# Denominators of linear attention by heads in column groups, their reciprocals spread over features by DMA through DRAM

## The chip, the cores and the metric

One core of one Trainium2 chip runs the kernel. The metric is device time in microseconds (us) of one execution, as the median over several runs; less is better. A profile taken by the hardware gives one execution in detail: its span goes from the first to the last instruction.

## What is computed

x is 2048 rows of 512 features, bfloat16. Two blocks follow each other, each with a layernorm ahead and x added behind: linear attention with 32 heads of 16 features, and a dense layer with 1792 hidden features and a relu.

```
qkv = (x @ wqkv)               # x after layernorm; 32 heads of Dh = 16
phi = lambda t: where(t > 0, t + 1, exp(t)) + 1e-6
pq, pk = phi(q), phi(k)
kv  = einsum("bhsd,bhse->bhde", pk, v)
z   = einsum("bhsd->bhd", pk)
num = einsum("bhqd,bhde->bhqe", pq, kv)
den = einsum("bhqd,bhd->bhq", pq, z)[..., None] + 1e-6
o   = num / den
h   = x + o @ wo
h2  = h + relu(layernorm(h) @ w1) @ w2
```

There is one denominator for each row and head, and it divides the 16 features of that head.

## The kernel before

The rows are cut into 16 tiles t of 128 rows, four of which make a block c of 512 rows (four blocks, c = 0 to 3; the text calls them blocks 1 to 4). All intermediates stay in SBUF. PSUM is one tensor `bk` of eight banks, and every step names its banks itself.

The kernel's body is a set of small functions `op_...`, and a text `ORDER` that lists them one after the other with their indices: `K.8.0` calls `op_K(8, 0)`, tile 8 into bank 0. The order of the words is the order in which each engine gets its instructions; there is no other scheduler. Engines run their own instructions in this order and wait for each other by semaphores. All DMAs are issued by SyncE (SP in the profile), also in this order, so a DMA whose data are late holds up the DMAs behind it.

The steps, with their lines in the kernel before:

- `lx`, `lk`, `lq`, `lv`, `lo`, `l1`, `l2` (L198, L201): loads of x and the weights. `warm` (L212): matmuls on zeros at the start. `S`, `A` (L215, L216): layernorm statistics on VectorE; `R` (L221, L222): one over the standard deviation by Ln and Exp on ScalarE; `N` (L229): the normalised tile, on VectorE.
- The normalised tile is needed transposed, in `lnT`: for tiles 0 to 5 by TensorE (`T`, L248) with a copy by ScalarE (`E`, L258) or VectorE (`V`, L261), for the others by a transposing DMA (`X`, L269).
- `K` (L277): keys of a tile; `F`, `U` (L295, L298): Exp and Relu from PSUM on ScalarE, two tiles at a time; `M`, `D` (L302, L305): minimum, add on VectorE, which give phi(k). `Q`, `qF`, `qU`, `qM`, `qD` do the same for the queries of a block, transposed (`pqT`), in four parts jb of 128 features, that is 8 heads.
- `G` (L329): x^T phi(k), summed over all tiles in banks 4 to 7; `z` (L337): the sums of phi(k); then `gD`, `gA` (L357, L354) copy G, `kv` (L362) multiplies with the value weights, `kx` (L370) masks it to heads, `m` (L374) multiplies with wo, `mD` (L380) copies it to `m_sb`. `zc` (L343) copies z; `zh` (L346) spreads it into `zhd`, 32 columns for each jb, of which 8 are the heads of that jb; `zr` (L351) spreads it into `zrep`, 128 columns, where each head's column stands 16 times.
- Denominators of block 1: `d4` (L386) makes four matmuls of 128x32 by 128x512, one for each jb, into four groups of 32 partitions of one bank: one row for each head. `dl4`, `dx4` (L392, L397) take one over it as Exp(-Ln). `rp` (L402) repeats it 16 times by four matmuls with `erep`, `rm` (L408) multiplies `pqT` with it from PSUM into `pqs`.
- Denominators of blocks 2 to 4: `d` (L415) makes one matmul of 128x128 by 128x512 for each jb with `zrep`, whose result stands repeated already; `dl`, `dx` (L418, L423) take one over it, one pass each for each jb, and `dm` (L426) multiplies `pqT` with it into `pqs`.
- `h` (L435): pqs times m_sb; `hD` (L441) adds x. `s`, `a`, `r`, `n` (L217, L218, L221, L236): statistics of the second layernorm; `t`, `x`: transposes by TensorE or by DMA (L270).
- `p` (L450): the hidden features f of a block; `pA`, `pD` (L456, L461): relu from two banks, on ScalarE or VectorE. `f` (L470): the second dense product of a tile; `fo` (L478): scaling and adding h; `fd` (L485): the store.

Around the change the order runs, on TensorE: the last Q and G, z, kv, m and the block 1 denominators, then h of block 1 mixed with Q of blocks 3 and 4, then p of block 1, and in it d of block 2. The d of blocks 3 and 4 come later, ahead of p of blocks 2 and 3.

Of the kernel before, what the change touches and what calls it, by code (L numbers as in the profile page):

```python
# [57 lines left out]
def kernel(  # L58
# [366 lines left out]
    def op_dm(c, jb):  # L425
        nc.vector.tensor_tensor(  # L426
            out=pqs[:, (c * KD + jb) % NQ, :], in0=pqT[c][:, jb, :], in1=rd[:, jb, :], op=ALU.mult
        )
# [92 lines left out]
```

## Time and profile before

| | us |
|---|---|
| median of 3 runs | 174.51 |
| the runs | 174.51, 175.42, 174.1 |
| span of the profiled execution | 173.1 |
| TensorE, VectorE, ScalarE, GpSimd busy in it | 165.8, 99.7, 72.3, 4.7 |
| first dense row of matmuls starts (K.0) | 8.71 |
| last matmul ends, by the chain | 170.06 |

The profile names no device time of its own for the profiled execution; what there is of it is the span, which lies 1.4 us under the median and 1.0 to 2.3 under the three runs. The granted TensorE clock was 1.000 over the span. PE is TensorE's matmuls, PEld its weight loads, DVE VectorE, ACT ScalarE, POOL GpSimd, SPq the issuing of DMAs by SyncE. A group's line has the source line, engine, operation, tiles and shapes, then total and mean time, then the idle time of its engine ahead of it and what ended that. Matmul durations (379 ns for 512 columns) overlap; their spacing in a dense row is read from the chain. The chain goes back from the last instruction to what released each step.

### The profile page before, as it was taken

Reading aid. Unit: us, or ns where it says so; the run is one execution under the profiler, and the core shown is the slowest. Engines: PE = TensorE matmul, PEld = TensorE weight load, DVE = VectorE, ACT = ScalarE, POOL = GpSimd, SP = SyncE. Lnnn points to the kernel's source line nnn. Section 1 sums busy time; section 2 is a strip of 40 time slices with the busy share of each in tenths; the row PEclk is TensorE's granted clock in tenths of the full one; section 3 lists DMA queues with packets and bytes.
Section 4 is the critical chain, followed back from the end, with each engine's and each line's share of the span. In section 5 each row is a group of like instructions: output and inputs, shape, how many; then the busy total and the mean of one; then the engine's idle time right before and its main releaser. Section 6 shows DMA issues by size and latency. Waiting matters only on the chain.

```text
span 173.1 us, 2263 instructions
## 1 busy us (share of the span) xinstructions
PE 165.8 (96%) x856; PEld 77.7 (45%) x872; DVE 99.7 (58%) x208; ACT 72.3 (42%) x112; POOL 4.7 (3%) x21
## 2 busy tenths in 40 slices
PE   7699989999999999999999999999999999999992
PEld 2244434446444544444444444444444444444551
DVE  3899965154799949796338089455769402500032
ACT  2499755666586794213057210006623000363100
POOL 7300000000000000000000000000000000000000
PEclk9999999999999999999999999999999999999999
DMA  5883456899000000002220000462001320010021
GB/s 139 280 307 61 77 132 152 255 364 360 4 0 0 4 0 0 0 0 61 61 64 30 0 2 0 108 78 91 0 0 30 65 60 0 30 62 0 0 80 45
DMA packets 19979, 13.00 MB, mean 75 GB/s; under 512 B 12544, under 2 KB 18816, under 8 KB 19968
## 3 DMA queue, kind: packets, MB, share of 16 engines
q1 hardware_dynamic: 19968, 12.85, 26.5%
q8 instruction: 7, 0.11, 0.3%
q14 instruction: 4, 0.03, 0.1%
HBM read 7.86 MB, written 2.10 MB: 58 GB/s over the span
## 4 chain that ended last, share of the span: by engine, by line
PE 85%; DVE 7%; DMA 5%; issue 1%; SPq 1%
PE bk L470 28%; PE bk L450 28%; PE bk L435 8%; PE bk L285 8%; PE bk L329 5%; PE bk L277 4%; DVE st L215 4%; DMA lnT<-h_nat 2%; DMA x_nat<-in_A_x_dram 2%; DVE h_nat L229 2%; PE bk L415 2%; PE bk L337 1%; DVE eb L302 1%; PE bk L374 1%; PE bk L248 1%
## 5 line engine op out<-in xcount | busy, mean ns | idle before, releaser
L450 PE MATMUL bk<-lnT,w_sb 128*128 128x512 bf16 x220 | 50.9, 379 | 0.2
L470 PE MATMUL bk<-w_sb,at 128*128 128x512 bf16 (+1 forms) x233 | 49.8, 366 | 0.3
L470 PEld LDWEIGHTS <-at 128*128 128x128 bf16 x238 | 23.3, 98 | 25.3
L450 PEld LDWEIGHTS <-w_sb 128*128 128x128 bf16 x224 | 21.9, 98 | 26.5
L456 ACT ACTIVATE at<-bk 128x1024 bf16<-128x1024 f32 x14 | 14.2, 1022 | 41.0 <-PE bk L450 22.3
L478 DVE SCALAR_TENSOR_TENSOR gT<-bk,rstd,h_nat 128x512 bf16<-128x512 f32 (+1 forms) x17 | 11.8, 716 | 30.4 <-PE bk L470 17.0
L461 DVE TENSOR_SCALAR at<-bk 128x1024 bf16<-128x1024 f32 x14 | 17.1, 1221 | 14.4 <-PE bk L450 14.4
L295 ACT ACTIVATE eb<-bk 128x1024 bf16<-128x1024 f32 (+1 forms) x18 | 16.6, 930 | 10.4 <-PE bk L277 6.1
L418 ACT ACTIVATE ld<-bk,eps 128x512 f32<-128x512 f32 x12 | 7.7, 693 | 27.7 <-PE bk L415 27.7
L298 ACT ACTIVATE rb<-bk 128x1024 bf16<-128x1024 f32 (+1 forms) x18 | 16.6, 927 | 1.3 <-DVE pqs L408 0.7
L277 PE MATMUL bk<-wk_sb,lnT 128*128 128x512 bf16 x64 | 15.3, 379 | 0.6 <-DMA lnT<-h_nat 0.6
L441 DVE TENSOR_TENSOR h_nat<-bk,x_nat 128x512 bf16<-128x512 f32 x16 | 10.7, 682 | 8.6 <-PE bk L435 8.6
L435 PE MATMUL bk<-m_sb,pqs 128*128 128x512 bf16 x62 | 15.2, 379 | 0.1
L285 PE MATMUL bk<-lnT,wq_sb 128*128 128x512 bf16 x61 | 14.7, 379 | 0.1
L329 PE MATMUL bk<-at,h_nat 128*128 128x512 bf16 x55 | 13.2, 379 | 0.1
L215 DVE BATCH_NORM_STATS2 st<-x_nat 128x6 f32<-128x512 bf16 x16 | 10.5, 680 | 2.7 <-DMA x_nat<-in_A_x_dram 2.7
L302 DVE TENSOR_SCALAR eb<-eb 128x1024 bf16<-128x1024 bf16 (+1 forms) x18 | 6.9, 389 | 7.0 <-ACT eb L295 7.0
L217 DVE BATCH_NORM_STATS2 st<-h_nat 128x6 f32<-128x512 bf16 x16 | 10.7, 683 | 0.2
L435 PEld LDWEIGHTS <-pqs 128*128 128x128 bf16 x64 | 6.3, 98 | 7.5
L277 PEld LDWEIGHTS <-lnT 128*128 128x128 bf16 x64 | 6.1, 98 | 7.9 <-DMA lnT<-h_nat 1.0
L329 PEld LDWEIGHTS <-h_nat 128*128 128x128 bf16 x64 | 6.2, 98 | 7.3
L285 PEld LDWEIGHTS <-wq_sb 128*128 128x128 bf16 x64 | 6.0, 98 | 6.9 <-issue 0.2
(63 smaller groups left out, 95.2 us busy)
## 6 DMA issues: line engine op xcount, KB each, us to landing
w_sb<-in_B_w_dram SPq DMA_DIRECT2D x4, 896.0 KB, 8.1
out_dram<-gT SPq DMA_DIRECT2D x15, 128.0 KB, 1.8
x_nat<-in_A_x_dram SPq DMA_DIRECT2D x2, 512.0 KB, 7.0
x_nat<-in_A_x_dram SPq DMA_DIRECT2D x3, 256.0 KB, 4.0
wk_sb<-in_A_wqkv_dram SPq DMA_DIRECT2D x2, 256.0 KB, 4.8
wq_sb<-in_A_wqkv_dram SPq DMA_DIRECT2D x2, 256.0 KB, 6.8
wv_sb<-in_A_wqkv_dram SPq DMA_DIRECT2D x2, 256.0 KB, 3.3
wo_sb<-in_A_wo_dram SPq DMA_DIRECT2D x2, 256.0 KB, 8.9
```

The source lines that it names most:

```text
L215: op_S = lambda t: nc.vector.bn_stats(out=st[:, t, :], in_=x_nat[:, t, :])
L277: nc.tensor.matmul(bk[:, b, :], lhsT=lnT[c][:, kd, j * P : (j + 1) * P], rhs=wk_sb[:, kd, :], start=(kd == 0), stop=(kd == KD - 1),)
L285: nc.tensor.matmul(bk[:, b, :], lhsT=wq_sb[:, kd, j * P : (j + 1) * P], rhs=lnT[c][:, kd, :], start=(kd == 0), stop=(kd == KD - 1),)
L295: nc.scalar.activation(out=buf(eb, kind, i, n), in_=bank(at_bank[kind, i], n), func=ACT.Exp)
L298: nc.scalar.activation(out=buf(rb, kind, i, n), in_=bank(at_bank[kind, i], n), func=ACT.Relu)
L329: nc.tensor.matmul(bk[:, KD + kd, :], lhsT=ln_nat[:, t, kd * P : (kd + 1) * P], rhs=pk(t)[:, 0, :], start=(t == 0), stop=(t == NT - 1),)
L435: nc.tensor.matmul(bk[:, b, :], lhsT=pqs[:, (c * KD + jb) % NQ, j * P : (j + 1) * P], rhs=m_sb[:, jb, :], start=(jb == 0), stop=(jb == KD ...
L450: nc.tensor.matmul(bk[:, b, :], lhsT=w1_sb[:, kd, f * P : (f + 1) * P], rhs=lnT[c][:, kd, :], start=(kd == 0), stop=(kd == KD - 1),)
L456: nc.scalar.activation(out=acts[c % 2][:, f : f + n, :], in_=bank(at_bank["p", c, f], n), func=ACT.Relu)
L461: nc.vector.tensor_scalar(out=acts[c % 2][:, f : f + n, :], in0=bank(at_bank["p", c, f], n), scalar1=0.0, scalar2=None, op0=ALU.max,)
L470: nc.tensor.matmul(bk[:, b, 0 : w * P], lhsT=acts[c % 2][:, f, j * P : (j + 1) * P], rhs=w2_sb[:, f, k * P : (k + w) * P], start=(f == 0), ...
L478: nc.vector.scalar_tensor_tensor(out=o_t[:, t % NO, cols], in0=bk[:, at_bank["f", t, k], 0 : w * P], scalar=rstd2[:, t : t + 1], in1=h_nat ...
```

## The change

For blocks 2 to 4 the four `d`, `dl`, `dx` of a block are replaced by one `d4`, one `dl4` and one `dx4`, as block 1 has them. The reciprocals go to `r4`, which is the memory of `wk_sb` (the key weights, no longer needed by then). Four DMAs `rw` write each head's row 16 times into a DRAM tensor `scr`, 128 KB each; two DMAs `rr` read two jb each, 256 KB, back into `rd`, now one row for each feature; and `dm` multiplies two jb at once. An `rr` waits on SP for the two `rw` that it reads. `zr` goes. Block 1 keeps `rp` and `rm`, with its four `rp` in two pairs. The order of all engines is written anew: tile 0 is normalised ahead of the statistics of tiles 2 and 3, X goes out in the order 6, 7, 9, 8, 13, 12, 10, 11, 15, 14, `lo` is loaded in part earlier and `lq` in part later, `lv` after all X, three of four z stand directly ahead of kv, d4.0 directly behind kv, some evictions change between ScalarE and VectorE (17 `pA` and 11 `pD` where there were 14 of each), and h of blocks 3 and 4 comes ahead of p of block 2. The loads of the first 4 us keep their order. The other functions that the diff adds are called nowhere in the order.

The diff, cut to what is spoken of (of the order, the first part and the end; line numbers of the later file are those of after):

```diff
-table const masks warm.9.7 lx.0.1 S.0 lx.1.1 S.1 A.0 A.1 lx.2.2 S.3 S.2 R.1.1 R.0.1 lx.4.2 lk.0.2 lk.2.2
-lx.6.2 A.3 A.2 N.0.2.2 N.0.0.2 N.1 R.2.2 N.2 N.3 warm.1.7 T.0.3.2.2 T.0.0.0.2 T.1.1 T.2.2 E.0.2.2 E.1 V.0.0.2
-T.3.3 E.2 E.3 K.0.0 S.4 S.5 A.4 A.5 K.1.1 K.3.3 K.2.2 F.0.1 R.4.2 U.0.1 F.1.1 S.6 S.7 M.0.1 A.7 A.6 N.4 R.6.2
-U.1.1 lx.8.4 T.4.0 D.0.1 G.0 M.1.1 N.5 N.7 T.5.1 E.4 U.2.1 F.2.1 E.5 F.3.1 U.3.1 K.4.0 D.1.1 S.9 N.6 S.8 G.1
-M.2.1 A.9 A.8 D.2.1 R.8.2 K.5.1 F.4.2 U.4.2 M.3.1 S.10 N.8 D.3.1 N.9 M.4.2 S.11 D.4.2 lq.2.2 lq.0.2 lx.12.4
-A.11 A.10 X.7 X.6 X.9 X.8 lv.0.2 G.2 K.7.3 K.6.2 G.3 F.6.2 R.10.2 U.6.2 S.12 S.13 M.6.2 N.11 N.10 A.13 A.12
-D.6.2 R.12.2 G.4 G.5 K.9.1 K.8.0 F.8.2 U.8.2 S.14 N.13 A.14 N.12 S.15 M.8.2 A.15 D.8.2 X.11 X.10 R.14.2 N.14
-N.15 lv.2.2 X.12 X.13 X.14 X.15 l1.0.2 l2.0.7 l2.7.7 lo.2.2 lo.0.2 l1.2.2 G.6 G.7 K.11.3 K.10.2 F.10.2 U.10.2
-G.8 G.9 K.12.0 K.13.1 F.12.2 U.12.2 M.10.2 D.10.2 G.10 K.14.2 K.15.3 F.14.2 M.12.2 M.14.2 D.12.2 Q.0.1.1
-Q.0.0.0 G.11 G.12 qF.0.0.2 qU.0.0.2 U.14.2 G.13 Q.0.3.1 Q.0.2.0 qM.0.0.2 D.14.2 qD.0.0.2 G.14 G.15 z.1.2
-qF.0.2.2 qU.0.2.2 gD.0.2 z.0.2 z.2.2 z.3.2 zc qM.0.2.2 gA.2.2 zr zh qD.0.2.2 Q.1.1.3 Q.1.0.2 qF.1.0.2 qU.1.0.2
-kv.1.4 kv.0.4 kv.2.4 kv.3.4 kx qM.1.0.2 Q.1.3.1 m.1.5 m.0.4 d4.0.3 m.3.7 m.2.6 Q.1.2.0 Q.2.0.2 dl4.0 mD.0.2
...
-d.1.1.5 qU.3.0.2 qF.3.0.2 e.0 d.1.0.4 d.1.3.7 qF.3.2.2 qU.3.2.2 dl.1.0 v.2 p.0.0.2 d.1.2.6 p.0.1.3 p.0.2.0
-p.0.3.1 dl.1.1 dx.1.0 dx.1.1 pD.0.0.2 p.0.4.2 p.0.5.3 qM.2.2.2 pD.0.2.2 p.0.6.0 p.0.7.1 dl.1.2 pD.0.4.2 dl.1.3
-dx.1.2 dx.1.3 r.0.4 p.0.8.2 p.0.9.3 pA.0.8.2 dm.1.2 dm.1.0 dm.1.3 dm.1.1 h.6.6 h.4.4 h.5.5 qM.3.2.2 qM.3.0.2
-pD.0.6.2 p.0.13.3 p.0.10.0 h.7.7 hD.6 f.2.6.0.7 p.0.11.1 p.0.12.2 hD.5 s.5 qM.2.0.2 f.1.5.0.7 s.6 hD.4 s.4
-pA.0.10.2 qD.2.0.2 a.4 pA.0.12.2 hD.7 a.5 f.3.7.0.7 f.1.5.7.7 n.4 qD.2.2.2 a.6 n.5 n.6 s.7 a.7 qD.3.0.2 n.7
...
+const lx.0.1 S.0 lx.1.1 A.0 table R.0.1 S.1 lx.2.2 N.0.0.2 N.0.2.2 A.1 S.2 R.1.1 warm.9.7 T.0.3.2.2 warm.1.7
+T.0.0.0.2 S.3 E.0.0.2 E.0.2.2 N.1 A.3 A.2 lx.4.2 lk.0.2 S.5 R.2.2 N.2 lk.2.2 T.1.3 E.1 A.5 S.4 K.0.0 T.2.7
+K.1.6 N.3 A.4 F.0.1 lx.6.2 E.2 T.3.4 R.4.2 M.0.1 S.7 N.5 K.2.2 T.5.7 E.3 U.0.1 S.6 N.4 D.0.1 A.6 lx.8.4 lq.0.2
+lo.2.2 lx.12.4 F.1.1 K.3.3 T.4.0 U.1.1 M.1.1 A.7 E.5 R.6.2 G.0 D.1.1 S.9 F.2.1 E.4 N.6 S.8 N.7 A.8 M.2.1 A.9
+F.3.1 M.3.1 U.2.1 R.8.2 X.6 K.5.1 G.1 U.3.1 K.4.0 D.2.1 N.9 F.4.2 U.4.2 G.2 K.6.2 D.3.1 S.12 S.13 N.8 M.4.2
+A.13 A.12 S.10 D.4.2 X.7 G.3 R.12.2 K.7.3 N.13 S.11 F.6.2 U.6.2 masks X.9 M.6.2 A.10 N.12 A.11 K.9.1 G.4 X.8
+X.13 lq.2.2 X.12 K.8.0 G.5 D.6.2 G.6 R.10.2 S.15 U.8.2 F.8.2 S.14 N.10 M.8.2 N.11 A.14 D.8.2 A.15 G.7 X.10
+K.13.1 K.12.0 R.14.2 X.11 G.8 K.10.2 K.11.3 F.12.2 U.12.2 U.10.2 F.10.2 N.14 N.15 M.10.2 Q.0.1.1 D.10.2 M.12.2
+X.15 Q.0.0.0 G.9 X.14 l2.0.7 lv.2.2 lo.0.2 K.14.2 G.10 K.15.3 lv.0.2 qF.0.0.2 qU.0.0.2 l1.0.2 G.11 Q.0.2.0
+Q.0.3.1 l2.7.7 l1.2.2 F.14.2 U.14.2 M.14.2 D.12.2 D.14.2 qM.0.0.2 qU.0.2.2 qF.0.2.2 z.2.2 G.12 G.13 G.14 G.15
+z.0.2 z.1.2 z.3.2 qM.0.2.2 qD.0.0.2 gD.0.2 qD.0.2.2 zc gA.2.2 kv.0.4 kv.1.4 kv.2.4 kv.3.4 zh d4.0.6 Q.1.0.2
+dl4.0 kx m.1.5 m.0.4 dx4.0 m.3.7 m.2.6 Q.1.1.3 mA.0.2 mD.2.2 rp.0.1.5 rp.0.0.4 qU.1.0.2 qF.1.0.2 Q.1.2.0
+rp.0.2.6 rp.0.3.7 Q.1.3.1 Q.2.1.3 rm.0.0.2 qF.1.2.2 rm.0.2.2 qM.1.0.2 qD.1.0.2 qM.1.2.2 h.2.4 Q.2.0.2 h.3.5
+qU.1.2.2 qD.1.2.2 hD.2 d4.1.0 h.0.7 Q.2.3.1 h.1.4 dl4.1 s.2 hD.3 s.3 dx4.1 qF.2.0.2 qU.2.0.2 a.2 a.3 n.3 t.3.6
+e.3 hD.0 n.2 hD.1 rw.1.1 rw.1.0 Q.2.2.0 qU.2.2.2 qF.2.2.2 s.0 s.1 a.0 Q.3.1.3 Q.3.0.2 t.2.4 rw.1.3 rw.1.2 n.0
+t.0.5 qU.3.0.2 qF.3.0.2 Q.3.3.1 qM.2.0.2 a.1 n.1 v.2 t.1.6 v.0 rr.1.0.2 v.1 qM.2.2.2 Q.3.2.0 qF.3.2.2 qD.2.0.2
+dm.1.0.2 p.0.1.3 rr.1.2.2 qU.3.2.2 p.0.0.2 dm.1.2.2 qM.3.0.2 qD.2.2.2 qM.3.2.2 h.6.5 p.0.3.1 p.0.2.0 d4.2.4
+r.0.4 pD.0.0.2 dl4.2 qD.3.2.2 qD.3.0.2 h.5.6 p.0.4.2 dx4.2 pA.0.2.2 d4.3.4 dl4.3 dx4.3 p.0.5.3 p.0.6.0 p.0.7.1
+h.7.7 h.4.4 rw.2.0 rw.3.2 rw.2.1 rw.2.2 pD.0.4.2 hD.5 pD.0.6.2 hD.7 rw.2.3 rr.2.0.2 rw.3.0 rw.3.1 rr.2.2.2
+hD.4 s.7 s.4 hD.6 a.7 p.0.8.2 p.0.9.3 p.0.10.0 f.3.7.0.7 pD.0.8.2 p.0.13.3 p.0.12.2 p.0.11.1 f.1.5.0.7
+dm.2.0.2 n.7 pD.0.10.2 dm.2.2.2 rw.3.3 x.7 rr.3.0.2 rr.3.2.2 pA.0.12.2 f.3.7.7.7 h.11.3 h.10.2 hD.11 hD.10
+s.10 s.5 a.4 dm.3.2.2 dm.3.0.2 a.5 s.6 fo.3 a.6 n.4 f.2.6.0.7 f.1.5.7.7 h.9.1 n.6 hD.9 n.5 x.6 f.2.6.7.7
+h.13.2 h.15.0 h.14.1 s.11 hD.14 fo.2 hD.15 f.0.4.0.7 h.8.3 h.12.6 x.4 x.5 p.1.13.1 p.1.12.0 pA.1.12.2 s.9 s.15
...
+f.12.4.0.7 fd.11 fd.10 f.15.7.0.14.0.2 f.13.5.0.7 f.14.6.0.7 f.13.5.7.7 f.12.4.7.7 f.14.6.7.7 fd.8 fo.15.0.2
+fo.12 fo.13 f.15.4.0.14.2.2 fo.14 fd.12 fd.13 fd.15.0.2 fd.14 fo.15.2.2 fd.15.2.2
 """
...
+    dram = ctx.enter_context(tc.tile_pool(name="dram", bufs=1, space=bass.MemoryType.DRAM))
...
     o_t = gT
+    r4 = wk_sb
+    scr = dram.tile([NCH, KD, P, CW], BF16, name="scr")
...
     def op_dx4(c):
-        nc.scalar.activation(out=rd[:, c % 2, :], in_=ld[:, c % 2, :], func=ACT.Exp, scale=-1.0)
+        nc.scalar.activation(out=r4[:, c, :], in_=ld[:, c % 2, :], func=ACT.Exp, scale=-1.0)
+
+    def op_rw(c, jb):
+        src = r4[jb * Q4 : jb * Q4 + P // DH, c, :].rearrange("q (o n) -> q o n", o=1)
+        nc.sync.dma_start(
+            out=scr[c, jb].rearrange("(q r) n -> q r n", r=DH),
+            in_=src.broadcast_to([P // DH, DH, CW]),
+        )
+
+    def op_rr(c, jb, n):
+        nc.sync.dma_start(
+            out=rd[:, jb : jb + n, :], in_=scr[c, jb : jb + n].rearrange("j p n -> p j n")
+        )
 
     def op_rp(c, jb, b):
         at_bank["rp", c, jb] = b
         rows = slice(jb * Q4, (jb + 1) * Q4)
         nc.tensor.matmul(
-            bk[:, b, :], lhsT=erep[rows, :], rhs=rd[rows, c % 2, :], start=True, stop=True
+            bk[:, b, :], lhsT=erep[rows, :], rhs=r4[rows, c, :], start=True, stop=True
...
-    def op_dm(c, jb):
+    def op_dm(c, jb, n=1):
+        i = (c * KD + jb) % NQ
         nc.vector.tensor_tensor(
-            out=pqs[:, (c * KD + jb) % NQ, :], in0=pqT[c][:, jb, :], in1=rd[:, jb, :], op=ALU.mult
+            out=pqs[:, i : i + n, :], in0=pqT[c][:, jb : jb + n, :], in1=rd[:, jb : jb + n, :],
+            op=ALU.mult,
         )
 
```

More of the change, by code (lines that the diff above doesn't have):

```diff
@@ L130 @@
     rstd = big.tile([P, NT], F32, name="rstd")
+    nmean = big.tile([P, NT], F32, name="nmean")
     st2 = big.tile([P, NT, nc.vector.BN_STATS_DIM], F32, name="st2")
@@ L222, in rstd_of, with op_ng, op_Np @@
         nc.scalar.activation(out=dst, in_=dst, func=ACT.Exp, scale=-0.5)
+    def op_ng(t, n):
+        nc.gpsimd.tensor_scalar(
+            out=nmean[:, t : t + n], in0=mv[:, t : t + n, 0], scalar1=-1.0, scalar2=None, op0=ALU.mult
+        )
+    def op_Np(t):
+        nc.gpsimd.tensor_scalar(
+            out=ln_nat[:, t, :], in0=x_nat[:, t, :],
+            scalar1=nmean[:, t : t + 1], scalar2=rstd[:, t : t + 1], op0=ALU.add, op1=ALU.mult,
+        )
     op_R = lambda t, n: rstd_of(rstd[:, t : t + n], mv[:, t : t + n, 1])
@@ L332, in op_G, with op_za, op_zf, op_z @@
             )
-    def op_z(jb, b):
+    def op_za(t):
+        first = pk(0, 2) if t == 2 else z_acc
+        nc.vector.tensor_tensor(out=z_acc, in0=first, in1=pk(t, 2), op=ALU.add)
+    def op_zf(t):
+        z0, z1 = z_acc[:, 0, :], z_acc[:, 1, :]
+        nc.vector.tensor_tensor(out=z0, in0=z0, in1=z1, op=ALU.add)
+        nc.vector.tensor_copy(out=acts[1][:, 4, :], in_=z0)
+        nc.vector.tensor_tensor(out=acts[1][:, 5, :], in0=z0, in1=acts[1][:, 4, :], op=ALU.subtract)
+    def op_z(jb, b, t0=0):
         at_bank["z"] = b
-        for t in range(NT):
+        parts = [pk(t)[:, 0, :] for t in range(t0, NT)] + [acts[1][:, i, :] for i in (4, 5) if t0]
+        for i, part in enumerate(parts):
             nc.tensor.matmul(
-                bk[:, b, jb : jb + 1], lhsT=pk(t)[:, 0, jb * P : (jb + 1) * P], rhs=ones[:],
-                start=(t == 0), stop=(t == NT - 1),
+                bk[:, b, jb : jb + 1], lhsT=part[:, jb * P : (jb + 1) * P], rhs=ones[:],
+                start=(i == 0), stop=(i == len(parts) - 1),
             )
@@ L396, in op_dx4 @@
     def op_dx4(c):
-        nc.scalar.activation(out=rd[:, c % 2, :], in_=ld[:, c % 2, :], func=ACT.Exp, scale=-1.0)
+        nc.scalar.activation(out=r4[:, c, :], in_=ld[:, c % 2, :], func=ACT.Exp, scale=-1.0)
[4 more added lines that the diff above has]
+            in_=src.broadcast_to([P // DH, DH, CW]),
+        )
+    def op_rr(c, jb, n):
+        nc.sync.dma_start(
+            out=rd[:, jb : jb + n, :], in_=scr[c, jb : jb + n].rearrange("j p n -> p j n")
+        )
     def op_rp(c, jb, b):
@@ L444, in op_hD, with op_p @@
         )
-    def op_p(c, f, b):
+    def op_p(c, f, b, s=0, n=1):
         at_bank["p", c, f] = b
+        cols = slice(s * CW // n, (s + 1) * CW // n)
         for kd in range(KD):
             nc.tensor.matmul(
-                bk[:, b, :], lhsT=w1_sb[:, kd, f * P : (f + 1) * P], rhs=lnT[c][:, kd, :],
+                bk[:, b, cols], lhsT=w1_sb[:, kd, f * P : (f + 1) * P], rhs=lnT[c][:, kd, cols],
                 start=(kd == 0), stop=(kd == KD - 1),
```

28 lines of the change are left out of this document (10 added, 18 removed).

## Prediction

> **What bounds the kernel now.** I read the page's shares first, then the chain in order of time, then the groups with shapes kept apart, last the DMA queue.
>
> ```profile
> PE 165.8 (96%) x856; PEld 77.7 (45%) x872; DVE 99.7 (58%) x208; ACT 72.3 (42%) x112; POOL 4.7 (3%) x21
> PE   7699989999999999999999999999999999999992
> ```
>
> TensorE is busy nearly everywhere; the other engines have room. So only three things move the end: TensorE work taken away, TensorE's idle stretches, and new ones. The chain shows what these are now.
>
> ```profile
> 18.36 0.17 SPq L269
> 18.54 0.05 issue
> 18.59 4.19 DMA lnT<-h_nat
> 22.78 0.05 issue
> 22.83 1.04 PE bk L277 x4
> ...
> 27.32 1.73 PE bk L329 x8
> ```
>
> From 22.83 us on the chain is TensorE alone until 170.06. 1.73/8 = 0.216 us is what one matmul of 512 columns costs in a dense row; a group of four is 0.863. TensorE's first dense row (K.0) starts at 8.71, K.9 starts at 21.25 and so ends at 22.11, and K.8 starts at 22.83 because the transposed tile of X.8 comes late: a hole of 0.72.
>
> ```profile
> L415 PE MATMUL bk<-pqT,zrep 128*128 128x512 bf16 x12 | 3.9, 379 | 0.0
> L386 PE MATMUL bk<-pqT,zhd 128*32 128x512 bf16 x4 | 0.4, 390 | 0.0
> L418 ACT ACTIVATE ld<-bk,eps 128x512 f32<-128x512 f32 x12 | 7.7, 693 | 27.7 <-PE bk L415 27.7
> L423 ACT ACTIVATE rd<-ld 128x512 bf16<-128x512 f32 x12 | 7.1, 637 | 0.2
> L426 DVE TENSOR_TENSOR pqs<-pqT,rd 128x512 bf16<-128x512 bf16 x12 | 4.5, 418 | 0.4 <-ACT rd L423 0.4
> L305 DVE TENSOR_TENSOR pqT<-rb,eb 128x1024 bf16<-128x1024 bf16 x8 | 5.4, 679 | 0.0
> ```
>
> L415 is what goes, L386 (block 1, already in column groups) is what comes three times more. The third view is the timeline around L386; columns are start and duration.
>
> ```profile
> 46.14 0.61 PE L374 MATMUL bk<-wo_sb,kvbd 128*128 128x512 bf16 x2
> 46.68 0.40 PE L386 MATMUL bk<-pqT,zhd 128*32 128x512 bf16 x4
> 47.01 0.60 PE L374 MATMUL bk<-wo_sb,kvbd 128*128 128x512 bf16 x2
> ```
>
> The two matmuls before it would let a dense row go on at 46.14 + 0.43 = 46.57. L386 starts at 46.68 and the next at 47.01: 0.11 of gap and 0.33 for four, 0.44 in all.
>
> ```profile
> x_nat<-in_A_x_dram SPq DMA_DIRECT2D x2, 128.0 KB, 2.3
> wv_sb<-in_A_wqkv_dram SPq DMA_DIRECT2D x2, 256.0 KB, 3.3
> out_dram<-gT SPq DMA_DIRECT2D x15, 128.0 KB, 1.8
> lnT<-h_nat SPq DMA_TRANSPOSE x10, 2.5
> ```
>
> These price the new transfers, from issue to landing.
>
> **The change, part by part.** Words such as K.8 are those of the order.
>
> *Matmuls of the denominators.* Off: 12 x 0.216 = 2.59 us on the path. On: 3 x 0.44 = 1.32. Gain 1.27; bounds 1.27 (gap each time) and 1.60 (0.33 each). I take 1.3. [...]
>
> *ScalarE and VectorE.* ScalarE loses 12 x 0.693 + 12 x 0.637 = 16.0 and gets 3 x (0.69 + 0.63) = 4.0, three more evictions at 1.02 and one of m_sb: about 8 less. VectorE swaps 12 x 0.418 for 6 multiplies of twice the width at 0.68 (L305's row) and loses three evictions, an m_sb copy and zrep: about 6 less. Neither is on the chain; I count nothing. TensorE's 96% covers it.
>
> *Start.* S.0, A.0 and N.0 now run before S.2, whose load landed at 5.46, so T.0 can start near 5.0 instead of 7.25. But K.0 needs wk_sb: its halves are issued at 2.65 and 3.13, in the same place as before, and land 4.2 and 5.3 later, at 6.85 and 8.43. So K.0 ends near 8.43 + 0.43 = 8.9 instead of 9.57, with T.2 and T.3 (0.22 each) still to come: gain 0.2. Bounds 0 (a load a little later) and 0.7 (9.57 less 8.9, if T.2 and T.3 too found an idle moment).
>
> *The hole before K.8.* I walked the new order with durations of this trace, back to back (512-wide ScalarE pass 0.48, 1024-wide 0.92, rstd pair 0.43; VectorE statistics 0.60, N 0.33). K.0 to G.2 stays dense to 16.7, each needed E, U or D ending 0.1 to 1 us ahead. X.8 goes out after N.8 near 18.2, no other load beside it (before, wv_sb was issued at 19.90 into its transit), lands after 2.5 at 20.7, and K.8 is wanted at 21.0. So the 0.72 goes; I take 0.7, bounds 0.7 and -0.7 (4.2 again: landed at 22.4, 1.4 late). What is late next is X.12, behind wq_sb's half, due 25.3, landing 24.6 (2.5) or 26.3.
>
> *G, z and kv.* Before, two Q groups (1.67) lay between z and kv. Now only three z groups (1.2) cover gT's copies, 0.2 to start and 1.22: they end 0.2 later, and kv follows 0.1 to 0.5 later than a dense row. Loss 0.35. d4.0 comes right behind kv and waits for z_sb and zhd, queued on VectorE behind the gT copy and one pqT add (0.60): loss 0.1, bounds 0 and 0.6.
>
> *Repeats of block 1.* The four matmuls of L402 cost 0.33 and a gap of 0.09 at one place. Now they are two pairs; each pays its gap, and a pair costs 0.22 to 0.33: 0.62 to 0.84 against 0.42. Loss 0.3.
>
> *Blocks 2 to 4 through DRAM.* New on SP: 12 writes of 128 KB and 6 reads of 256 KB, 18 issues of about 0.55. For blocks 3 and 4 more than ten groups of 0.86 lie between d4 and the first h, over 9 us; I cost these at nothing, that work hides them. The transposes x.7, x.6, x.4, x.5 are queued behind them on SP and end about 1 us before p.1 wants them. Block 2 is tight. After d4.1, ten groups and four transposes, 8.63 + 0.88 = 9.5 us, run before h.6 needs pqs. In that time: L392 and L397 with starts 1.4; four issues 0.55 apart, the last begun at 1.4 + 0.1 + 1.65 = 3.15; its landing 1.8 to 2.3 later, near 5.2; the second read, issued there, lands 2.7 to 3.3 later, near 8.2; the multiply 0.68 gives 8.9 and a start. VectorE's own queue (two v, qM, qD and the first multiply) reaches the last multiply no sooner than 9.0, which ends near 9.7, so h.6 waits 0.2. Bounds: 0 and, with a write at 4.2 (wk_sb's first half) and a read at 6.9 (the slower wq_sb), 3.15 + 4.2 + 6.9 + 0.7 = 14.95, that is 5.5. I take 0.2: no other load moves at that time, as for the rows of wv_sb and out. Queued behind the waiting multiply are the mins and adds of blocks 3 and 4 and the first eviction of p, needed by p.0.4 some 1.5 us after they are ready.
>
> [...] No row here shows a repeated source.
>
> *The end.* The last half tile and its store are ordered as before, 170.06 to 173.1: nothing.
>
> **Sum.** -1.3 - 0.2 - 0.7 + 0.35 + 0.1 + 0.3 + 0.2 = -1.25: the span goes from 173.1 to 171.85. The median of the runs, 174.51, stands 1.4 over the profiled span; with the same 1.4 the time is 173.3, 0.7% less.
>
> **Rivals.**
>
> *B, the order holds better than I walk it.* Pairs at 0.22 and gaps hidden, d4 at 0.33, gT's copies and zhd in time: the three losses of 0.75 go and the gain of d4 is 1.6, span 170.8 less the 0.2 of h.6: 170.6 to 170.8, time 172.1. For it: one engine at 96% with others below 60% gives an order much room. Against: the gap of 0.11 is in the trace at each change of tile shape.
>
> *C, the round trip ends last: slower.* The chain then goes through the read into h.6. Without its 0.2 the rest gains 1.45; it decides from a wait of 1.45 on, that is when the second read's landing comes 10.25 us after d4.1 instead of 8.2. At the upper bound of 5.5 the span is 173.1 - 1.45 + 5.5 = 177.15, time 178.5; the middle of the case is 176.5. For it: loads in the first 10 us took 4.2 to 6.9 for 256 KB, and two landings are in series. Against: those shared the engines with 2 MB, these with little.
>
> *D, the first 30 us keep a hole.* X.8 or X.12 at 4.2: 1.4 more, span 173.25, time 174.7, no change. For it: one transfer of ten did so. Against: a load lay beside it.
>
> That the column groups do not run side by side is excluded by L386's 0.33.
>
> **How the numbers follow.** Forecast 0.50 (own range 172.4 to 174.2), B 0.25, C 0.15, D 0.10. The predicted time is the forecast's 173.3. About 1% is what a measurement of this kernel can tell from no change, so the marks are 172.8 and 176.3. Faster: all of B and 0.13 of the forecast, 0.38. Slower: 0.08, half of C and a little of D with more than one hole. Within: 0.54. The range 171.9 to 175.2 takes in most of B, all of D and a third of C, and leaves out about 0.15.
>
> **What would show it.** Right: L386's line x16 at 0.33 to 0.44 a group in the chain; K.0's row ending near 8.9; no DMA in the chain near 20 to 26; a VectorE or DMA piece of at most 0.3 before the fifth h group (near 61). Wrong: a DMA piece rd<-scr in the chain, over 1 us of TensorE idle anywhere between 9 and 168, landings of the writes over 3 us, or of the reads over 4.

## The result, and the profile after

The changed kernel takes 188.83 us (median of 4 runs, 187.39 to 189.58), the kernel before beside it 174.31 (4 runs, 173.97 to 175.42). The ratio is 1.081, interval 1.075 to 1.086: slower by 8%, where 173.3 was predicted. In some executions of a kernel the granted clock is lower and the time longer (e5: 175.81 us at 0.99, 172.78 to 174.93 at 1.00); the ratios and intervals in this text leave the slow ones out. The profiled execution took 187.39 and its span is 185.7.

From the page of the changed kernel: busy times, TensorE's share and granted clock in 40 slices of 4.64 us, the chain by engine, and two groups.

```profile
PE 166.8 (90%) x857; PEld 76.4 (41%) x872; DVE 94.3 (51%) x197; ACT 65.7 (35%) x98; POOL 4.7 (3%) x21
...
PE   7699899999999419999559989999999999999993
...
PEclk9999999999999966999999999999999999999999
...
PE 63%; DMA 19%; DVE 7%; ACT 5%; SPq 3%; issue 2%
...
L475 PE MATMUL bk<-m_sb,pqs 128*128 128x512 bf16 x61 | 16.3, 392 | 9.5 <-DVE pqs L465 9.3
...
L465 DVE TENSOR_TENSOR pqs<-pqT,rd 128x1024 bf16<-128x1024 bf16 x6 | 4.1, 691 | 16.0 <-DMA rd<-scr 16.0
```

ScalarE and VectorE have less to do, as the change meant (65.7 against 72.3, 94.3 against 99.7), and TensorE has the same. But its row of nines now has two dents, in slices 14 and 15 and in slices 20 and 21, and the clock row has a dent behind the first, in slices 15 and 16. The multiply with the reciprocals (L465) waited 16.0 us for reads of `rd`, and the h matmuls (L475) waited 9.3 us for the multiply. In the kernel before both columns were near nothing: that multiply waited 0.4 in all.

The chain of the changed kernel in order of time, cut to the pieces around the waits (start, duration, what):

```profile
18.20 3.38 DMA lnT<-h_nat
...
52.42 0.36 PE bk L412 x4
...
52.80 0.69 ACT ld L418
...
53.52 0.64 ACT wk_sb L423
...
55.79 1.76 SPq L427
...
57.60 8.67 DMA scr<-wk_sb
...
66.28 2.79 DMA rd<-scr
...
69.09 0.70 DVE pqs L465
...
69.84 1.03 PE bk L475 x2
70.88 2.83 PE bk L491 x8
...
83.80 4.87 DMA rd<-scr
...
89.58 6.77 DMA scr<-wk_sb
...
96.42 3.26 DMA rd<-scr
```

The round trip of block 2 can be read off step by step: d4.1 at 52.42, Ln and Exp, four issues, then a write that lands 8.67 us after its issue, a read of 2.79, the multiply, and h.6. The start of the first issue, the read and the multiply cost what was priced; the issues (0.67 to 1.76 against 0.55) and above all the write did not. Blocks 3 and 4 then make a second stretch of the same kind.

What it costs TensorE is in a table by stretch. Columns: stretch, length, busy time and number of PE, PEld, DVE, ACT, POOL, then the granted clock, the DMA share and GB/s.

```profile
9.00:62.40 53.40, 52.51 (x334) 24.93 (x336) 38.27 (x90) 40.23 (x59) 0.00 (x0) 1.00 0.51 141
62.40:66.20 3.80, 0.00 (x0) 0.00 (x0) 0.00 (x0) 0.63 (x3) 0.00 (x0) 0.99 0.54 100
66.20:69.84 3.64, 0.64 (x1) 0.13 (x3) 1.44 (x3) 0.00 (x0) 0.00 (x0) 0.50 0.29 83
69.84:73.00 3.16, 3.16 (x8) 1.16 (x9) 3.16 (x6) 0.00 (x0) 0.00 (x0) 0.50 0.00 0
73.00:84.00 11.00, 10.95 (x56) 4.62 (x55) 7.18 (x11) 3.45 (x5) 0.00 (x0) 1.00 0.28 46
84.00:96.00 12.00, 8.16 (x37) 3.36 (x37) 3.70 (x6) 1.02 (x1) 0.00 (x0) 1.00 0.62 99
```

The matmuls of that time, from the timeline of TensorE:

```profile
60.50 1.89 PE L491 MATMUL bk<-lnT,w_sb 128*128 128x512 bf16 x8
68.25 0.64 PE L475 MATMUL bk<-m_sb,pqs 128*128 128x512 bf16 x1 [5.85 <-DVE pqs L465]
69.84 1.03 PE L475 MATMUL bk<-m_sb,pqs 128*128 128x512 bf16 x2 [0.96 <-DVE pqs L465]
```

h.6 is four matmuls, two for each half of `pqs`. TensorE ends a piece of p at 62.39 and stands until the first half is there, runs two of the four (the record of one is missing), and stands again until 69.84: 3.80 + 3.00 = 6.8 us by the windows, where the kernel before had no such gap. After 3.8 us of it the granted clock goes from 0.99 to 0.50, until 73.00. So the last two of h.6 and the eight of p behind them take 1.03 + 2.83 = 3.86 us in the chain; ten such matmuls in a dense row are 2.16, and 1.7 us are lost to the clock. Together, the twelve matmuls behind 62.39 end at 73.71; in a dense row they would take 2.59, so block 2 costs 8.7 us here.

Between 84 and 96 TensorE idles another 3.8. There the first multiply of block 3 holds VectorE's queue for 4.30 us, and the eviction of p behind it runs only at 89.57, for which the dense product waits 1.4; h waits 2.5 more for the second multiply.

### The profile page after: what moved, and what is told of

Read it like the earlier page. It is cut to its first block, busy times and chain, and to the rows that moved or that the text cites. A ratio compares the mean times of both kernels' runs of the same rounds, so it can differ in the third digit from the quotient of the medians.

```text
span 185.7 us, 2260 instructions
## 1 busy us (share of the span) xinstructions
PE 166.8 (90%) x857; PEld 76.4 (41%) x872; DVE 94.3 (51%) x197; ACT 65.7 (35%) x98; POOL 4.7 (3%) x21
## 4 chain that ended last, share of the span: by engine, by line
PE 63%; DMA 19%; DVE 7%; ACT 5%; SPq 3%; issue 2%
PE bk L491 22%; PE bk L511 21%; DMA scr<-wk_sb 8%; DMA rd<-scr 6%; PE bk L344 5%; PE bk L300 5%; PE bk L292 4%; PE bk L475 3%; DMA wk_sb<-in_A_wqkv_dram 3%; DMA lnT<-h_nat 2%; SPq L427 2%; DVE h_nat L481 2%; DVE pqs L465 1%; ACT eb L310 1%; ACT rb L313 1%
## 5 line engine op out<-in xcount | busy, mean ns | idle before, releaser
L491 PE MATMUL bk<-lnT,w_sb 128*128 128x512 bf16 x218 | 52.5, 386 | 0.7 <-issue 0.4
L511 PE MATMUL bk<-w_sb,at 128*128 128x512 bf16 (+1 forms) x237 | 51.6, 367 | 1.5 <-DVE at L502 1.4
L497 ACT ACTIVATE at<-bk 128x1024 bf16<-128x1024 f32 x17 | 17.3, 1022 | 76.3 <-PE bk L491 76.3
L475 PE MATMUL bk<-m_sb,pqs 128*128 128x512 bf16 x61 | 16.3, 392 | 9.5 <-DVE pqs L465 9.3
L502 DVE TENSOR_SCALAR at<-bk 128x1024 bf16<-128x1024 f32 x11 | 13.4, 1219 | 20.6 <-PE bk L491 20.6
L292 PE MATMUL bk<-wk_sb,lnT 128*128 128x512 bf16 x64 | 16.2, 380 | 1.2 <-DMA wk_sb<-in_A_wqkv_dram 0.7
L300 PE MATMUL bk<-lnT,wq_sb 128*128 128x512 bf16 x62 | 15.4, 380 | 0.2 <-issue 0.2
L475 PEld LDWEIGHTS <-pqs 128*128 128x128 bf16 x64 | 5.9, 98 | 18.0 <-DVE pqs L465 10.8
L465 DVE TENSOR_TENSOR pqs<-pqT,rd 128x1024 bf16<-128x1024 bf16 x6 | 4.1, 691 | 16.0 <-DMA rd<-scr 16.0
```

What stands on the lines that cost most here:

```text
L292: nc.tensor.matmul(bk[:, b, :], lhsT=lnT[c][:, kd, j * P : (j + 1) * P], rhs=wk_sb[:, kd, :], start=(kd == 0), stop=(kd == KD - 1),)
L300: nc.tensor.matmul(bk[:, b, :], lhsT=wq_sb[:, kd, j * P : (j + 1) * P], rhs=lnT[c][:, kd, :], start=(kd == 0), stop=(kd == KD - 1),)
L475: nc.tensor.matmul(bk[:, b, :], lhsT=pqs[:, (c * KD + jb) % NQ, j * P : (j + 1) * P], rhs=m_sb[:, jb, :], start=(jb == 0), stop=(jb == KD ...
L491: nc.tensor.matmul(bk[:, b, cols], lhsT=w1_sb[:, kd, f * P : (f + 1) * P], rhs=lnT[c][:, kd, cols], start=(kd == 0), stop=(kd == KD - 1),)
L497: nc.scalar.activation(out=acts[c % 2][:, f : f + n, :], in_=bank(at_bank["p", c, f], n), func=ACT.Relu)
L502: nc.vector.tensor_scalar(out=acts[c % 2][:, f : f + n, :], in0=bank(at_bank["p", c, f], n), scalar1=0.0, scalar2=None, op0=ALU.max,)
```

## The experiments

Five explanations were to be told apart. P: each write takes its data from 8 neighbouring partitions, and these deliver slowly. E: with 8 rows in the source only part of the 16 DMA engines work. L: two landings in series are too long as such. O: the new order loses by itself. W: the order's thin start lets the clock fall. The kernel before runs beside each experiment; on the chips of these runs its median was 175.58 (e1 to e4), 176.09 (e5 to e8) and 175.91 (e9 to e12), so ratios, not times, are compared across rows. A row with one run has no interval. In the table, "wait for rd" is the time that VectorE's multiplies waited for a read.

| run | rows of one write, repeats | time, us (runs) | ratio to before | span of the profile | wait for rd |
|---|---|---|---|---|---|
| the change | 8 neighbours, x16 | 188.83 (4) | 1.081 [1.075, 1.086] | 185.7 | 16.0 |
| e1 | no writes | 174.21 (4) | 0.990 [0.985, 0.994] | 172.6 | 0 |
| e2 | 128, x1 | 176.42 (1) | | 174.7 | 0 |
| e3 | 8 of 32, every fourth, x16 | 175.12 (1) | | 173.4 | 0 |
| e4, e11 | 32 neighbours, x4 | 174.75 (10), 174.02 (4) | 0.993 [0.989, 0.996], 0.988 [0.983, 0.993] | 172.1, 173.4 | 0 |
| e5, e12 | one write of 128, x4 | 173.75 (6), 174.6 (10) | 0.985 [0.980, 0.990], 0.991 [0.987, 0.995] | 172.2 (e5) | 0 (e5) |
| e6 | 16 neighbours, x8 | 177.07 (1) | | 175.3 | 2.4 |
| e7 | as e4, more zero matmuls | 175.99 (12) | 1.000 [0.997, 1.003] | 174.3 | 1.0 |
| e8 | as e5, order of before | 178.96 (6) | 1.012 [1.006, 1.017] | 177.3 | 5.0 |
| e9 | block 2 as e4, 3 and 4 as the change | 179.56 (1) | | 177.8 | 7.8 |
| e10 | 3 and 4 as e4, block 2 as the change | 182.18 (1) | | 180.5 | 6.8 |

### e1: the new order without the writes

```diff
-        src = r4[jb * Q4 : jb * Q4 + P // DH, c, :].rearrange("q (o n) -> q o n", o=1)
-        nc.sync.dma_start(
-            out=scr[c, jb].rearrange("(q r) n -> q r n", r=DH),
-            in_=src.broadcast_to([P // DH, DH, CW]),
-        )
...
-            out=rd[:, jb : jb + n, :], in_=scr[c, jb : jb + n].rearrange("j p n -> p j n")
+            out=rd[:, jb : jb + n, :],
+            in_=xf[jb * P : (jb + n) * P, :].rearrange("(j p) n -> p j n", p=P),
```

The reads fetch rows of x, so the reciprocals are left out of the result.

> Leaves the 12 writes out and lets the 6 reads fetch rows of x in place of the reciprocals, so no read waits for a write; order, d4 and reads stay. If the loss comes from the writes (theory P, few source partitions; theory E, few engines; theory L, the length of a round trip), VectorE no longer waits for rd and the span falls from 185.7 to 171 to 173, under before's 173.1. If the new order itself loses (theory O), the span stays over 177 and TensorE keeps idle stretches of over 2 us between 60 and 100.

Measured: 174.21 us, ratio 0.990, span 172.6. No multiply waits. The timeline of e1 shows both multiplies of block 2 together, with no idle time put down to a read:

```profile
62.23 1.29 DVE L466 TENSOR_TENSOR pqs<-pqT,rd 128x1024 bf16<-128x1024 bf16 x2
```

So the new order, its matmuls, reads and multiplies do not lose; O falls, and the whole loss comes in with the writes.

### e2: the same bytes written from 128 partitions

```diff
-        src = r4[jb * Q4 : jb * Q4 + P // DH, c, :].rearrange("q (o n) -> q o n", o=1)
-        nc.sync.dma_start(
-            out=scr[c, jb].rearrange("(q r) n -> q r n", r=DH),
-            in_=src.broadcast_to([P // DH, DH, CW]),
-        )
+        nc.sync.dma_start(out=scr[c, jb], in_=r4[:, c, :])
```

Each write takes all of `r4` as it stands, so the repeating of a head's row is left out.

> Same 12 writes of 128 KB at the same places, each still awaited by its read, but each from 128 partitions once, not from 8 partitions 16 times (wrong values). P and E: a write moves in about 0.4 us instead of some 2.6 (128 KB at the 50 GB/s seen), the four of block 2 land within 3 us of the last issue, the reads no longer start 7 to 12 us after dx4, span 172 to 174. L: the two landings in series stay, DVE waits for rd of over 3 us at block 2, span over 178.

Measured in one run: span 174.7, no wait for rd; the writes land in 1.8 us (the median) and the reads in 2.8 to 3.8. The number of transfers, their bytes and the two landings in series are those of the change, so L falls. The span is 2.1 over e1's, with a granted clock of 0.987 where e1 has 1.000, and in its chain four K matmuls take 1.71 us at 10.33 and 1.35 at 12.46, where four at 14.03 take 0.86: part of it is the fall at the start that W speaks of (e7).

### e3: 8 rows again, every fourth of 32 partitions

The matrix for the denominators now holds each head's column four times, so the 8 heads of a jb stand in 32 rows of `r4`, and each write takes every fourth of them.

```diff
-                bk[jb * Q4 : (jb + 1) * Q4, b, :], lhsT=zhd[:, jb, :], rhs=pqT[c][:, jb, :],
+                bk[jb * Q4 : (jb + 1) * Q4, b, :], lhsT=(zhd4 if c else zhd)[:, jb, :], rhs=pqT[c][:, jb, :],
...
-        src = r4[jb * Q4 : jb * Q4 + P // DH, c, :].rearrange("q (o n) -> q o n", o=1)
+        src = r4[jb * Q4 : (jb + 1) * Q4 : 4, c, :].rearrange("q (o n) -> q o n", o=1)
```

> Each head's denominator is made four times (columns of the group), and a write takes every fourth partition of its 32, so again 8 rows, 16 times each, by as many engines as before, but rows spread over 32 partitions. P: the writes speed up by well over 1.5 (over 80 GB/s instead of 50) and the span falls to 172 to 176. E: rate stays near 50 GB/s and the span stays at 184 to 187.

Measured in one run: 175.12 us, span 173.4, no wait for rd. The two views that decide are the DMA rows of block 2's writes, each a window cut in 40 slices: the busy share of the 16 engines, and GB/s. First the change, 54 to 62 us:

```profile
DMA  0000000033444334443344444444444443454834
GB/s 0 0 0 0 0 0 0 0 61 46 51 51 56 46 46 51 51 56 46 46 56 46 56 46 46 51 46 56 46 46 51 46 51 67 113 102 56 138 41 51
```

Then e3, 55.7 to 59.5 us:

```profile
DMA  0000000000000001545654415454645454555444
GB/s 0 0 0 0 0 0 0 0 0 0 0 0 0 0 0 54 194 172 183 216 205 172 173 43 205 172 194 172 237 172 183 151 194 172 205 205 194 172 162 173
```

The busy share of the engines is 0.3 to 0.4 in the change and mostly 0.4 to 0.5 in e3, so in both they stand about half the time or more, which fits E. But with the same eight rows the change moves 50 GB/s and e3 some 180. Rows, repeats, bytes and the DRAM side are equal; only the distance of the source partitions differs, and the matrix that fills them. P stands; E may be true of the engines but is not the price. The four writes of a block are 0.52 MB, and at 50 GB/s they take 10.5 us; in the chain they last from 55.6 to 66.27, which is 10.7.

### e4, e11: 32 neighbouring rows, each repeated 4 times

```diff
-        src = r4[jb * Q4 : jb * Q4 + P // DH, c, :].rearrange("q (o n) -> q o n", o=1)
+        src = r4[jb * Q4 : (jb + 1) * Q4, c, :].rearrange("q (o n) -> q o n", o=1)
...
-            out=scr[c, jb].rearrange("(q r) n -> q r n", r=DH),
-            in_=src.broadcast_to([P // DH, DH, CW]),
+            out=scr[c, jb].rearrange("(q r) n -> q r n", r=4),
+            in_=src.broadcast_to([Q4, 4, CW]),
```

(and `zhd4` as in e3)

> As the kernel with four copies of each denominator, but a write takes all 32 partitions of its group, 4 times each: same bytes and places, right values. P and E: the rate is over 120 GB/s, h of block 2 waits under 1.5 us, span 171.5 to 174. If the step-4 kernel stays slow and this one is fast, E holds; if both are fast, P. L: span over 178 here as well.

Measured: 174.75 us (10 runs), ratio 0.993 [0.989, 0.996], and in e11, which runs it again, 174.02, ratio 0.988 [0.983, 0.993]. The profiled execution of e4 took 173.77 with a span of 172.1. Its DMA rows, 54.4 to 57.6 us:

```profile
DMA  0000000000000000258999976799998867999999
GB/s 0 0 0 0 0 0 0 0 0 0 0 0 0 0 0 0 51 154 218 230 205 205 230 179 154 192 230 218 230 205 192 192 141 180 230 230 205 205 205 230
```

The engines are busy for 0.6 to 0.9 of the time, and the rate is about 205 GB/s: a far higher share than in e3 (0.4 to 0.5), and little more rate (180 there). A write now lands in 2.4 us and a read in 2.9 (medians). The chain of e4 has no DMA after the transposes:

```profile
18.55 3.32 DMA lnT<-h_nat
...
42.68 0.92 PE bk L400 x16
43.59 0.33 PE bk L424 x4
43.92 0.97 PE bk L307 x4
...
60.90 1.73 PE bk L503 x8
62.63 0.86 PE bk L487 x4
```

The last line is h.6, straight behind p, at 62.63. In the change its first two matmuls ran at 68.25 and its last two at 69.84.

### e5, e12: one write for a block, from all 128 partitions

```diff
-        src = r4[jb * Q4 : jb * Q4 + P // DH, c, :].rearrange("q (o n) -> q o n", o=1)
+        src = r4[:, c, :].rearrange("q (o n) -> q o n", o=1)
...
-            out=scr[c, jb].rearrange("(q r) n -> q r n", r=DH),
-            in_=src.broadcast_to([P // DH, DH, CW]),
+            out=scr[c].rearrange("j (q r) n -> (j q) r n", r=4),
+            in_=src.broadcast_to([P, 4, CW]),
```

(and `zhd4` as in e3; `rw` once for each block in the order)

> As the kernel that reads all 32 partitions of a group, but one write of 512 KB for each block, from all 128 partitions 4 times each, in place of four of 128 KB; right values. P: a rate near that of loads (over 280 GB/s), nothing waits in h of block 2, span 171.5 to 172.5, no gain over four writes, because those were hidden already. L, or a cost of SP's issues: 0.5 or more below the four-write kernel's 172.1.

Measured: 173.75 us (6 runs), ratio 0.985 [0.980, 0.990]; the three writes of 512 KB and the six reads land in 2.7 to 3.6 us, with a median of 3.2 (of the reads alone 3.0). e12 ran it again beside e11:

> The one-write kernel once more on the same chip as the four-write kernel: ratio 0.980 to 0.990 if the first result holds; 0.990 to 0.996, as the four-write kernel, if that was due to the chip.

> The four-write kernel from 32 partitions once more, beside the one-write kernel on the same chip: ratio 0.989 to 0.996 as the first time, 0.3 to 0.8 percent behind the one-write kernel if the latter's 0.9851 was due to its form, equal to it if it was due to the chip.

174.6 us, ratio 0.991 [0.987, 0.995] for e12 and 0.988 [0.983, 0.993] for e11: one write and four do not differ by more than the runs scatter. Both beat the kernel before by about 1% and the change by some 8%.

### e6: 16 neighbouring rows, each repeated 8 times

```diff
-        src = r4[jb * Q4 : jb * Q4 + P // DH, c, :].rearrange("q (o n) -> q o n", o=1)
+        src = r4[jb * Q4 : jb * Q4 + 16, c, :].rearrange("q (o n) -> q o n", o=1)
...
-            out=scr[c, jb].rearrange("(q r) n -> q r n", r=DH),
-            in_=src.broadcast_to([P // DH, DH, CW]),
+            out=scr[c, jb].rearrange("(q r) n -> q r n", r=8),
+            in_=src.broadcast_to([16, 8, CW]),
```

Of the 16 rows 8 hold no head, so the features do not get the reciprocals of their heads.

> The changed kernel with each write from 16 neighbouring partitions 8 times each (8 of them hold no head, so wrong values): 16 outer rows where 8 were, twice as many partitions, same places, bytes and waits. P: the rate doubles from 50 to about 100 GB/s, four writes of block 2 take some 5 us in place of 10, VectorE still waits for rd, 1 to 3 us at block 2, span 174 to 179. E: with 16 outer rows all engines take part and the rate is over 170 GB/s, as with 32 rows; no wait, span 172 to 173.

Measured in one run: 177.07 us, span 175.3, a wait for rd of 2.4 and TensorE's of 2.1 ahead of h.6. Its DMA rows, 54 to 61 us:

```profile
DMA  0000000000001679888898898889867797988793
GB/s 0 0 0 0 0 0 0 0 0 0 0 0 29 111 99 105 94 99 94 100 105 100 99 111 88 94 129 246 234 146 117 99 111 94 105 99 99 105 187 82
```

This is the mirror image of e3: the 16 engines are busy for 0.8 to 0.9 of the time, and up to the first read at 59.5 they move about 100 GB/s (88 to 117 in most slices, 129 to 246 between 58.55 and 59.25). In these runs the rate goes with the number of neighbouring partitions (8: 50, 16: 100, 32: about 205), not with the busy share of the engines (0.8 to 0.9 at 100 here, 0.4 to 0.5 at 180 in e3).

### e7: a warmer start

```diff
-T.0.0.0.2 S.3 E.0.0.2 E.0.2.2 N.1 A.3 A.2 lx.4.2 lk.0.2 S.5 R.2.2 N.2 lk.2.2 T.1.3 E.1 A.5 S.4 K.0.0 T.2.7
+T.0.0.0.2 warm.4.7 S.3 E.0.0.2 E.0.2.2 N.1 A.3 A.2 lx.4.2 lk.0.2 S.5 R.2.2 N.2 lk.2.2 T.1.3 warm.3.7 E.1 A.5 S.4 K.0.0 T.2.7
```

(and all of e4)

> The 32-partition kernel with 7 more matmuls on zeros in TensorE's idle time before K.0 (4 behind tile 0's transposes, 3 behind tile 1's). Theory W: the new order's thin start lets the granted clock fall in some runs (0.56 over 8.7 to 12 us in the step-4 kernel, 1.2 us lost); then the clock stays 1.000 in every run and the median falls by 0.3 to 1.2 us against the kernel without them. Rival: the clock falls independently of these matmuls, same median within 0.3, and the matmuls cost up to 0.3 where they run late.

Measured: 175.99 us (12 runs), ratio 1.000 [0.997, 1.003]. The clock did what W wanted: 0.998 to 1.000 in all twelve runs, where single executions of e2 and e3 had 0.987 and 0.989 (in e3, 0.66 between 8 and 13 us). The time did not follow; it is no better than e4's. In the profiled execution two waits have grown, from its chain:

```profile
18.46 4.60 DMA lnT<-h_nat
...
57.60 4.04 DMA scr<-wk_sb
...
61.66 2.65 DMA rd<-scr
```

The transposed tile of X.8 comes 1.2 us later than in e4 and TensorE waits 1.72 for it; block 2's write took 4.04 and h.6 waits 0.8. Why matmuls on zeros at 6 to 8 us should lengthen these was not tried. As a way to gain time W has failed.

### e8: one write for a block, in the order of before

The order is that of before, with `d4`, `dl4`, `dx4`, one `rw` and two `rr` where `d`, `dl` and `dx` stood, and two `dm` in place of four; from the block 2 part:

```diff
-d.1.1.5 qU.3.0.2 qF.3.0.2 e.0 d.1.0.4 d.1.3.7 qF.3.2.2 qU.3.2.2 dl.1.0 v.2 p.0.0.2 d.1.2.6 p.0.1.3 p.0.2.0
-p.0.3.1 dl.1.1 dx.1.0 dx.1.1 pD.0.0.2 p.0.4.2 p.0.5.3 qM.2.2.2 pD.0.2.2 p.0.6.0 p.0.7.1 dl.1.2 pD.0.4.2 dl.1.3
-dx.1.2 dx.1.3 r.0.4 p.0.8.2 p.0.9.3 pA.0.8.2 dm.1.2 dm.1.0 dm.1.3 dm.1.1 h.6.6 h.4.4 h.5.5 qM.3.2.2 qM.3.0.2
+d4.1.5 qU.3.0.2 qF.3.0.2 e.0 qF.3.2.2 qU.3.2.2 dl4.1 dx4.1 rw.1.0 rr.1.0.2 rr.1.2.2 v.2 p.0.0.2 p.0.1.3 p.0.2.0
+p.0.3.1 pD.0.0.2 p.0.4.2 p.0.5.3 qM.2.2.2 pD.0.2.2 p.0.6.0 p.0.7.1 pD.0.4.2 r.0.4 p.0.8.2 p.0.9.3 pA.0.8.2
+dm.1.0.2 dm.1.2.2 h.6.6 h.4.4 h.5.5 qM.3.2.2 qM.3.0.2
```

> The order of before, with column groups, one write and two reads for blocks 2 to 4 (from all 128 partitions) in place of d, dl, dx. If the saving is that of the column groups (my 1.3 us) and the new order brings about nothing, the span is 171.5 to 172.5 and the ratio to before 0.990 to 0.996. If the new order brings it, the span is 173 or more, by waits of h for the round trip, which this order gives 7 to 9 us.

Measured: 178.96 us (6 runs), ratio 1.012 [1.006, 1.017], span 177.3: slower than before, and the expected gain did not come. The chain of e8 goes through the round trip once for each block (shown: the first row of K, then the round trips of blocks 2 and 3; block 4's follows with 3.19 and 3.39):

```profile
9.28 5.52 PE bk L298 x16
...
65.63 3.26 DMA scr<-wk_sb
...
68.90 2.73 DMA rd<-scr
...
90.58 3.20 DMA scr<-wk_sb
...
93.79 2.94 DMA rd<-scr
```

Even with writes from all partitions the way through DRAM is 6 us and more, and the old order has no such room between d and h. Not all of the 1.2% is this: in the profiled execution d4.0 starts at 48.90 against 46.75 before, 2.1 us later, before any reciprocal goes to DRAM. Nearly all of that is in the first row of K: its 16 matmuls take 5.52 us, 0.345 each, where 16 in a dense row take 3.45, 0.216 each, though the clock reads 1.00 between 9.5 and 65. The cause was not looked for. The other 2.1 us of the longer span come behind d4.0. What is sure is that the wait appears in this order at 3.2 us a write and not in the new one.

### e9 and e10: which blocks lose

```diff
-        src = r4[jb * Q4 : jb * Q4 + P // DH, c, :].rearrange("q (o n) -> q o n", o=1)
+        rows = Q4 if c == 1 else P // DH
+        a0 = jb * Q4
+        src = (r4[a0 : a0 + Q4, c, :] if c == 1 else r4[a0 : a0 + P // DH, c, :])
+        src = src.rearrange("q (o n) -> q o n", o=1)
```

(e9; e10 has `c > 1` in the place of `c == 1`)

> The changed kernel with only block 2's writes from all 32 partitions; blocks 3 and 4 keep 8 neighbouring ones. TensorE's idle time in the changed kernel was 6.2 us at block 2's h and about 4.7 us between 84 and 108. P with my costing of blocks 3 and 4 at nothing: the span returns to 172 to 173. If the writes of blocks 3 and 4 are late by themselves: 176 to 178, with VectorE waiting for rd at their multiplies.

> The other half: blocks 3 and 4 from 32 partitions, block 2 from 8 neighbouring ones. If block 2's wait is a loss of its own: 6 to 8 us over the repaired kernel, span 178 to 180, all of the wait at block 2's h and the granted clock under 0.8 behind it. If the late start of SP on blocks 3 and 4 came from block 2, the sum of both halves' losses is well over the 13.6 between the changed and the repaired kernel or under it by over 2.

Measured, one run each: with only block 2 mended the span is 177.8, with only blocks 3 and 4 mended 180.5. Over e4's 172.1 the slow writes of blocks 3 and 4 cost 5.7 and those of block 2 cost 8.4; together 14.1, against the 13.6 of the whole change over e4. e4 ran on another chip; over the 173.4 of e11, the same kernel on the chip of e9 and e10, the two are 4.4 and 7.1. Either way both parts lose by themselves, block 2 the most. From the chain of e9:

```profile
72.33 6.65 DMA scr<-wk_sb
...
79.05 6.38 DMA rd<-scr
...
85.45 0.70 DVE pqs L480
```

The read too is slow, 6.38 in place of 2.9. It was issued while block 4's writes were on their way; that they held it up is what the order of the issues suggests, but it was not tried by itself.

## Why the prediction was wrong

The mechanism of rival C (the chain goes through the read into h.6) is what happened; it had been given a chance of 0.15, and its upper end of 178.5 was still 10 us short. Of the other terms the matmuls and the repeats came out near their price, the start only in part, and two did not: the hole before K.8 stayed, and the loss at z, kv and d4.0 did not come. Step by step, read in e4, where the writes are mended, against before:

| term | predicted | measured | from |
|---|---|---|---|
| matmuls of the denominators | -1.3 | -1.27 | 0.33 and 0.11 more in the group behind (0.97 for 0.86), three times, against 2.59 |
| start | -0.2 | -0.19 in the change, +0.16 in e4 | K.0's row ends at 8.94 and 9.29, before at 9.57, but two groups of transposes (0.44) that stood ahead of it before still follow; wk_sb landed at 8.30 and 8.64 |
| hole before K.8 | -0.7 | -0.1 | X.8 landed in 3.3 (before 4.2); TensorE's idle is 0.46 (before 0.55) |
| z, kv, d4.0 | +0.45 | 0 | z, kv, d4.0 follow without a gap, 42.68 and 43.59 |
| repeats of block 1 | +0.3 | +0.44 | 0.32 and a gap of 0.11 for each pair, 0.86 against 0.42 |
| h.6 waits | +0.2 | 0 in e4; 7.6 in the change, 8.7 with the p at half clock behind it | between the p ahead of h.6 and h.6's end 0.86 in e4, 62.39 to 70.88 in the change |
| blocks 3 and 4 | nothing | 0 in e4; 4.4 to 5.7 in e9 | e9 against e11 and e4 |

Without the two last rows -1.45 was predicted; in e4 the last matmul ends at 168.88 against 170.06 before, -1.2. That this is near is partly luck: two errors cancel (the hole stayed, the kv loss did not come), and the rows of e4 add up to -0.8, so 0.4 of its gain was traced to no place.

**The step that failed.** "Four issues 0.55 apart, the last begun at 1.4 + 0.1 + 1.65 = 3.15; its landing 1.8 to 2.3 later." The last write began 57.60 - 52.78 = 4.8 us after d4.1, since the three issues ahead of it had become long (0.85, 0.67 and 1.76 us), and landed 8.67 later. The price was taken from `x_nat` and `out_dram`, which have 128 KB as well but move it to or from 128 partitions. The writes of the change take theirs from 8. As durations 2.3 and 2.6 us (128 KB at 50 GB/s) hardly differ; the error is what they consist of. An estimate from e2's rows: at the 350 GB/s that it reaches in bursts, 128 KB are 0.4 us of transfer in a landing of 1.8 (the median), and the bursts of block 2's four writes follow each other within 2 us, from 57.5 to 59.5; the writes of the change move about 50 GB/s all through and queue, 4 x 2.6 = 10.5 us. The upper bound erred likewise: 4.2 us from a load at the start bounds one transfer, not four in a line.

**"I cost these at nothing, that work hides them."** The same sum makes 10.5 us for block 3 and 10.5 for block 4, one behind the other through one SP queue: 21 us against the 9 us named as cover. e9 shows the price, 4.4 to 5.7. The cover was right for a 6 us round trip and was not held against a transfer time in series. The queue effect was seen in the text (evictions behind a waiting multiply) for block 2, where it was priced by a wait of 0.2, and is what costs TensorE 1.4 us at block 3.

**The place of the source.** No term of the sum has it, and the rate goes with it: from eight rows four partitions apart e3 moves 180 GB/s, and the change 50 from eight neighbouring ones. The busy share of the 16 engines does not go with the rate: it is 0.3 to 0.4 in the change, mostly 0.4 to 0.5 in e3, and mostly 0.6 to 0.9 in e4 (205 GB/s) and e6 (100).

**The tests named in advance** worked: the piece rd<-scr in the chain, more than 1 us of idle TensorE and landings over 3 us were to show the forecast wrong, and all three stand in the profile.

**The hole before K.8.** The reason given (no load beside the transfer) is refuted: no load lay beside X.8 in e4 between 18.5 and 21.5 and it still took 3.3, and 4.6 in e7. In each of three executions (before, the change, e4) a transfer of 0.02 MB of the instruction queue lay in its transit, between 20.5 and 21.5 us. That is a coincidence in time and was not tried; the cause stays open.
